# Products with V as 64-row tiles of the weight array, two key halves at a time, with the half query chunk widened to 128 columns

## The chip, the cores and the metric

One core of one Trainium2 chip. The metric is the device time of one launch in microseconds (us); lower is better. The engines are TensorE (PE; its weight loads are listed apart as PEld), VectorE (DVE), ScalarE (ACT), GpSimd (POOL) and the queue engine SP.

## The reference

Attention with one added to the softmax's denominator, over 8 batches x 12 heads, 448 tokens, head size 64; then a soft mixture of experts over all 3584 tokens with 8 experts of 4 slots each.

```python
# attention, per batch and head
scores = scale * q @ k.T                       # scale = 1/8
m = max(scores, axis=-1)
e = exp(scores - m)
x = (e / (sum(e) + exp(-m) + 1e-9)) @ v        # tokens go on as rows [3584, 768]
# soft MoE
logits = x @ phi                               # [3584, 32]
d = softmax(logits, axis=0); c = softmax(logits, axis=1)
slot_in = d.T @ x                              # [32, 768], 4 slots per expert
slot_out = relu(slot_in[e] @ w1[e]) @ w2[e]    # w1 768x1024, w2 1024x768
out = c @ slot_out
```

## The kernel before

Heads are worked in 48 pairs (`NPAIR`); a pair n holds two heads, hl = 0 in partitions 0 to 63 and hl = 1 in 64 to 127. The 448 tokens make three chunks of 128 and a half chunk of 64, for keys (index i) and for queries (index u). The order of all engines' work is the order in which the Python code issues it (`manual_schedule`): each engine runs its own part of that order strictly in sequence, and waits on the semaphore of whoever made its input or still uses its buffer.

For each pair there are these pieces:

- `T` (L241): 28 transposes of 64x64 turn q and k of a later pair into `ps_t`, copied out by ACT or DVE.
- `A` (L274): scores with queries on the partitions, only for the row maximum; `ps_a`, reduced by DVE (L287, L307). Seven reductions a pair.
- `W1` to `W3` (L310 to L349): once in three pairs the negated maxima are transposed to a row `mT`, and exp(-m) is made in `ec`.
- `Bk(n, i)` (L352): scores with keys on the partitions, plus the bias -m by a second matmul of 64 rows (L370, L399), then exp on ACT (L372, L402) into one of five SBUF buffers `e2` (both heads of a chunk side by side, 448 columns each) or, for the half chunk, into `e1`. The matmuls of the two heads use rows 0 to 63 and 64 to 127 of the array and stand alternately with those of `A`.
- `AV(n, i, qs)` (L421): the product with V. The exponentials are the weights (128 keys x 128 queries), V with a column of ones is the moving operand (65 columns). Per pair 4 key chunks x 4 query chunks x 2 heads = 32 matmuls; the half query chunk gives matmuls with 64 weight columns, the half key chunk stacks both heads' 64 keys on 128 rows with zeros in `vp` for the other head. All goes into one PSUM bank (`ps_av`, 7 x 65 columns).
- `N1` (L443): ACT copies `ps_av` to `ubuf`. `N2` (L452): DVE adds exp(-m) and takes the reciprocal, POOL multiplies in three operations (L469, L479, L480) into `x`.
- `PX` (L494): four matmuls with the identity transpose x; ACT copies them out (L507).
- `P(b)` (L516): the MoE's part for a batch, in six functions that the table `post` hangs into later half steps.

In the main loop a step s has two halves. The first: Bk(s,0), Bk(s,1), each with one `A` between; then AV(s-1) for key chunks 2 and 3, and the half query chunk of AV(s-1); N1. The second: Bk(s,2), Bk(s,3) with `A`; T(s+6); AV(s) for key chunks 0 and 1; PX(s-2); N2. The first three pairs are issued by hand, by the words of `ramp`; the MoE's expert layers and the output follow after the loop. PSUM has 8 banks: 3 in `psA`, 4 in `psB` (scores, `T`, `PX`), 1 in `psV` (`ps_av`).

POOL issues the loads of q, k, v and of the expert weights between its own work (`slot_loads`, `load_half`, `load_rows`); the tables `half_at`, `rows_at` and `stage_at` say in which step.

Of the kernel before, what the change touches and what calls it, by code (L numbers as in the profile page):

```python
# [24 lines left out]
HG = 6  # L25
NP = 3
# [5 lines left out]
def kernel(  # L32
# [37 lines left out]
    ident2 = const.tile([128, 128], BF16, name="ident2")  # L70
    ones = const.tile([128, 2], BF16, name="ones")
    sel = const.tile([128, HG], BF16, name="sel")
    phi_sb = const.tile([128, KC, NS], BF16, name="phi_sb")
    halfm = const.tile([128, 2], F32, name="halfm")
# [6 lines left out]
    sizes = [("nq0", 2 * NP * S), ("nq1", 2 * NP * S), ("nv", NATV), ("qk6", 2 * S), ("wm1", 512),  # L81
             ("qk0", 2 * S), ("qk1", 2 * S), ("qk2", 2 * S), ("wm0", 512), ("xTa", 4 * 512), ("qk3", 2 * S),
             ("vp0", VPN), ("x0", 4 * DD), ("qk4", 2 * S), ("qk5", 2 * S), ("e2", NE * 2 * S), ("e1", S),
# [12 lines left out]
    e1_t = part("e1", 0, S)  # L96
    vp = [part(f"vp{i}", 0, VPN).rearrange("p (h i d) -> p h i d", h=HG, i=4) for i in range(2)]
    wm = [part(f"wm{i}", 0, 512).rearrange("p (i c) -> p i c", i=4) for i in range(2)]
# [57 lines left out]

    with ExitStack() as at:
# [4 lines left out]
        psB = pool("psB", 4, space=PSUM)  # L162
# [3 lines left out]
        ubuf = pu.tile([128, 2, 7 * W65], F32, name="ubuf")  # L166
# [30 lines left out]
        for t in wm:  # L197
            nc.vector.memset(t, 0.0)
# [9 lines left out]
        for t, x in ((halfm, 1.0), (nhalfm, -1.0)):  # L208
            nc.vector.memset(t, 0.0)
            for hl in range(2):  # L210
                nc.vector.memset(t[64 - 64 * hl:128 - 64 * hl, hl:hl + 1], x)
        nc.vector.memset(ones, 1.0)
        nc.vector.memset(ones[64:128, 1:2], 0.0)
# [4 lines left out]
        for h in range(2):  # L218
            nc.vector.tensor_add(ident2[:, 64 * h:64 * h + 64], ident[:, 0:64], ident[:, 64:128])
# [11 lines left out]
        mx, ngm, ec, mT, eT, av, us = {}, {}, {}, {}, {}, {}, {}  # L231
# [9 lines left out]
        def T(n):  # L241
            g, pl = divmod(n, NP)
            first = n < NP * NP
            ps = psB.tile([128, 2, S], BF16, tag="b", name="ps_t")
# [65 lines left out]
        def W1(g):  # L310
            w, m = wm[g % 2], mx[g]
            l0, l1 = mpl(g)
            nm = psm.tile([128, 21], BF16, tag="ngm", name="ngm")
            neg = lambda o, s: nc.gpsimd.tensor_scalar(o, s, -1.0, None, op0=ALU.mult)
            cols = lambda t: t[:, 0:3 * HG].rearrange("p (i c) -> p i c", i=3)[:, :, 2 * l0:2 * l1]

            o = w[:, 3, :].rearrange("p (d c) -> p d c", d=2)[:, :, 2 * l0:2 * l1]
            nc.gpsimd.tensor_mul(
                o.rearrange("p d (l h) -> p d l h", h=2),
                m[:, 3 * HG + l0:3 * HG + l1].unsqueeze(1).unsqueeze(3).to_broadcast([128, 2, l1 - l0, 2]),  # L320
                nhalfm.unsqueeze(1).unsqueeze(1).to_broadcast([128, 2, l1 - l0, 2]))
            o = w[:, 0:3, :].rearrange("p i (d c) -> p i d c", d=2)[:, :, :, 2 * l0:2 * l1]
            neg(o, cols(m).unsqueeze(2).to_broadcast([128, 3, 2, 2 * (l1 - l0)]))
            if l1 - l0 == NP:
                neg(nm, m)
            else:
                nc.gpsimd.memset(nm, 0.0)
                neg(cols(nm), cols(m))
                neg(nm[:, 3 * HG + l0:3 * HG + l1], m[:, 3 * HG + l0:3 * HG + l1])
            ngm[g] = nm  # L330

        def W2(g):
            w = wm[g % 2]
            ps = pb_("ps_m")
            for i in range(3):
                nc.tensor.matmul(ps[:, i * 128:(i + 1) * 128], w[:, i, :], ident, start=True, stop=True)
            nc.tensor.matmul(ps[:, 384:448], w[:, 3, :], ident2[:, 0:64], start=True, stop=True)
            st["ps_m"] = ps

        def W3(g):  # L340
            t = psm.tile([128, S], BF16, tag="mT", name="mT")
            nc.scalar.copy(t, st["ps_m"][:, 0:S])
            mT[g] = t
            e = psm.tile([128, NP, 7], F32, tag="ec", name="ec", bufs=3)
            nc.scalar.activation(e[:, :, 0:6].rearrange("p l (i h) -> p i l h", i=3),
                                 ngm[g][:, 0:18].rearrange("p (i l h) -> p i l h", i=3, h=2),
                                 AF.Exp, scale=scale)
            nc.scalar.activation(e[:, :, 6], ngm[g][:, 18:21], AF.Exp, scale=scale)
            ec[g] = e  # L349


        def Bk(n, i, c=0, mix=False):  # L352
# [3 lines left out]
            rs = [slice(0, 64), slice(64, 128)]  # L356
            if i < 3 and mix and runs and runs[0][1] < 3:

                e = e2_t[st["e2"] % NE]
                st["e2"] += 1  # L360
                cols = slice(i * 128, (i + 1) * 128)
                a0, a1 = A(*runs.pop(0), steps=True)
                pss = {}

                def score(hl):
                    pss[hl] = pb_("ps_b")
                    nc.tensor.matmul(pss[hl][:, 0:S], t[rs[hl], 1, cols], t[rs[hl], 0, :], start=True, stop=False)  # L367

                def bias(hl):
                    nc.tensor.matmul(pss[hl][:, 0:S], sel[rs[hl], 2 * pl + hl:2 * pl + hl + 1].to_broadcast([64, 128]),  # L370
                                     mT[mg(n)][rs[hl], :], start=False, stop=True)
                    nc.scalar.activation(e[:, hl, :], pss[hl][:, 0:S], AF.Exp, scale=scale)  # L372
                    eT[n, i, hl] = e[:, hl, :]

                a0()
                score(1)
                score(0)
                bias(1)
                bias(0)
                a1()  # L380
                return
            if i < 3:
                pss = [pb_("ps_b") for _ in range(2)]
                outs = [p[:, 0:S] for p in pss]
                cols = slice(i * 128, (i + 1) * 128)
                e = e2_t[st["e2"] % NE]
                st["e2"] += 1
                es = [e[:, hl, :] for hl in range(2)]
            else:
                pss = [pb_("ps_b")]  # L390
                outs = [pss[0][r, 0:S] for r in rs]
                cols = slice(384, 448)
                es = [e1_t]
            m = cols.stop - cols.start
            for hl in range(2):
                nc.tensor.matmul(outs[hl], t[rs[hl], 1, cols], t[rs[hl], 0, :], start=True, stop=False)  # L396
            As(c)
            for hl in range(2):
                nc.tensor.matmul(outs[hl], sel[rs[hl], 2 * pl + hl:2 * pl + hl + 1].to_broadcast([64, m]), mT[mg(n)][rs[hl], :],  # L399
                                 start=False, stop=True)  # L400
            for p, e in zip(pss, es):
                nc.scalar.activation(e, p[:, 0:S], AF.Exp, scale=scale)  # L402
            for hl in range(2):
                eT[n, i, hl] = es[hl % len(es)]
# [10 lines left out]
        def av_tile(n):  # L415

            if n >= NPAIR - 3:
                return psA.tile([128, 512], F32, tag="a", name="ps_av")
# [613 lines left out]
```

## Time and profile before

| | |
|---|---|
| median of 3 runs | 299.27 us (299.16, 299.27 and 453.81) |
| span of the profiled execution | 299.0 us |
| PE busy | 271.4 us, 91% |
| DVE busy | 249.7 us, 84% |
| ACT busy | 249.8 us, 84% |
| POOL busy | 195.9 us, 66% |
| granted PE clock | 1.00 up to 270 us, 0.60 and 0.50 in the last 29 us |
| DMA | 58.7 MB in 299 us |

The span is the time from the first to the last instruction in the one execution that the profiler took; it is 0.3 us below the median. A group's line in the profile gives the source line, engine, operation, output<-input with shapes (for PE rows*columns of the weight tile first), the count, the busy time, the mean length of one in ns and the idle time before it. A line of the timeline gives the start in us, the time from the first start to the last end, and what ran. A matmul's length includes the way through the array, so that matmuls overlap: 448 columns last 0.35 us, but follow each other at 0.19 us.

### The profile page before, as it was taken

The numbers are of one execution on the slowest core, as the hardware profiler recorded it, in microseconds if no ns is written. First come the engines' busy times: TensorE is split into PE (matmuls) and PEld (weight loads), VectorE is DVE, ScalarE is ACT, GpSimd is POOL, SyncE is SP. The second block draws the span as 40 slices with busy tenths as digits, with TensorE's granted clock in tenths as the row PEclk, the third lists the DMA queues.
The fourth block names the chain that finished last, engine by engine and source line by source line (L and its number), as shares of the span: only waits on it lengthen the run. The fifth ranks groups of instructions, "written<-read, shape, count | busy, mean of one in ns | idle before, by whom it ended". The sixth has DMA issues, their size and how long they took to land.

```text
span 299.0 us, 12398 instructions
## 1 busy us (share of the span) xinstructions
PE 271.4 (91%) x5174; PEld 162.5 (54%) x5174; DVE 249.7 (84%) x581; ACT 249.8 (84%) x559; POOL 195.9 (66%) x391
## 2 busy tenths in 40 slices
PE   5999899999999999999899999999999999996820
PEld 4445456566666566566556666656665555652100
DVE  5899799999999989999889999998999675537930
ACT  3569999999899989998989899989999987337820
POOL 8792887979696979887879697978686633000000
PEclk9999999999999999999999999999999999997555
DMA  7999998999999999999999999999799989908997
GB/s 132 147 143 208 149 138 138 188 165 188 185 204 179 184 176 202 163 182 182 202 159 184 176 199 152 196 183 196 125 150 187 213 185 263 344 10 318 380 453 322
DMA packets 47015, 58.67 MB, mean 196 GB/s; under 512 B 2800, under 2 KB 39920, under 8 KB 46704
## 3 DMA queue, kind: packets, MB, share of 16 engines
q0 software_dynamic: 40304, 42.29, 89.6%
q1 hardware_dynamic: 6656, 15.60, 13.8%
q8 instruction: 40, 0.66, 0.8%
q14 instruction: 15, 0.12, 0.1%
HBM read 89.16 MB, written 15.14 MB: 349 GB/s over the span
## 4 chain that ended last, share of the span: by engine, by line
PE 68%; ACT 10%; DVE 6%; POOL 6%; issue 4%; DMA 2%; DVEq 0%; POOLq 0%; ACTq 0%
PE ps_av L436 15%; PE ps_a L285 10%; PE ps_b L367 7%; PE ps_b L370 7%; PE ps_t L256 5%; PE ps_b L396 5%; PE ps_x L501 3%; PE ps_b L399 3%; ACT W L402 2%; PE ps_o L925 2%; DVE mx L298 2%; PE ps_s L623 2%; PE ps_h L862 2%; PE ps_so L882 2%; ACT W L263 2%
## 5 line engine op out<-in xcount | busy, mean ns | idle before, releaser
L287 DVE TENSOR_REDUCE mx<-ps_a 128x1 f32<-128x448 f32 x250 | 137.3, 613 | 4.6 <-PE ps_a L285 3.5
L372 ACT ACTIVATE W<-ps_b 128x448 bf16<-128x448 f32 x250 | 120.4, 574 | 0.0
L285 PE MATMUL ps_a<-W 64*128 64x448 bf16 x250 | 80.9, 352 | 0.0
L367 PE MATMUL ps_b<-W 64*128 64x448 bf16 x250 | 70.5, 352 | 1.1
L436 PE MATMUL ps_av<-W 128*128 128x65 bf16 (+1 forms) x1536 | 64.9, 196 | 2.2 <-issue 1.6
L436 PEld LDWEIGHTS <-W 128*128 128x128 bf16 (+1 forms) x1536 | 50.5, 100 | 30.2 <-issue 26.4
L370 PE MATMUL ps_b<-mT,sel 64*128 64x448 bf16 x250 | 66.5, 350 | 0.0
L469 POOL TENSOR_TENSOR W<-ubuf,rec 128x384 bf16<-128x384 f32 x44 | 36.3, 824 | 35.7 <-ACT W L507 19.3
L402 ACT ACTIVATE W<-ps_b 128x448 bf16<-128x448 f32 x86 | 46.1, 574 | 2.0 <-PE ps_b L399 2.0
L256 PEld LDWEIGHTS <-W 64*64 64x64 bf16 x1344 | 29.3, 112 | 12.7 <-issue 4.3
L507 ACT CAST W<-ps_x 128x512 bf16<-128x512 f32 x47 | 28.6, 608 | 7.4 <-PE ps_x L501 7.2
L256 PE MATMUL ps_t<-ident,W 64*64 64x64 bf16 x1330 | 30.6, 195 | 2.4 <-ACT W L215 1.4
L307 DVE TENSOR_REDUCE mx<-ps_a 128x1 f32<-128x448 f32 x48 | 29.5, 615 | 1.4 <-PE ps_a L304 1.4
L285 PEld LDWEIGHTS <-W 64*128 64x128 bf16 x250 | 23.4, 94 | 9.8
L114 POOL DMA_DIRECT2D W<-in_moe_w_dram x30 | 22.6, 755 | 7.9 <-PE ps_b L399 7.8
L370 PEld LDWEIGHTS <-sel 64*128 64x128 bf16 x250 | 19.6, 94 | 14.4 <-issue 5.6
L396 PE MATMUL ps_b<-W 64*64 64x448 bf16 (+1 forms) x134 | 27.1, 374 | 0.3
L449 ACT COPY ubuf<-ps_av 128x455 f32<-128x455 f32 x44 | 25.1, 571 | 0.8 <-POOL W L408 0.6
L399 PE MATMUL ps_b<-mT,sel 64*64 64x448 bf16 (+1 forms) x134 | 25.1, 354 | 0.1
L263 ACT COPY W<-ps_t 128x896 bf16<-128x896 bf16 x21 | 19.5, 927 | 6.5 <-PE ps_t L256 6.5
L298 DVE TENSOR_REDUCE mx<-ps_a 128x1 f32<-128x448 f32 x38 | 21.1, 616 | 1.9 <-PE ps_a L294 1.9
L480 POOL TENSOR_TENSOR W<-ubuf,rec 128x128 bf16<-128x128 f32 x44 | 17.5, 398 | 3.7
(156 smaller groups left out, 446.6 us busy)
## 6 DMA issues: line engine op xcount, KB each, us to landing
W<-in_moe_w_dram POOLq DMA_DIRECT2D x24, 768.0 KB, 9.9
W<-in_v_dram POOLq DMA_DIRECT2D x32, 192.0 KB, 6.5
out_dram<-W SPq DMA_DIRECT2D x2, 2688.0 KB, 10.0
W<-in_q_dram POOLq DMA_DIRECT2D x15, 336.0 KB, 6.3
W<-in_k_dram POOLq DMA_DIRECT2D x15, 336.0 KB, 7.5
stage<-in_moe_w_dram POOLq DMA_DIRECT2D x4, 768.0 KB, 9.6
W<-stage SPq DMA_DIRECT2D x4, 576.0 KB, 7.3
out_dram<-W SPq DMA_DIRECT2D x6, 384.0 KB, 3.0
```

Source lines behind the costliest of these rows:

```text
L256: nc.tensor.transpose(o, src[r, pl, tok * D:(tok + 1) * D], ident[r, r])
L285: nc.tensor.matmul(ps[:, 0:S], t[r, 0, i * 128:(i + 1) * 128], t[r, 1, :], start=True, stop=True)
L287: nc.vector.reduce_max(m[:, c:c + 1], ps[:, 0:S], axis=AX.X)
L307: nc.vector.reduce_max(mx[g][:, c:c + 1], ps[:, 0:S], axis=AX.X)
L367: nc.tensor.matmul(pss[hl][:, 0:S], t[rs[hl], 1, cols], t[rs[hl], 0, :], start=True, stop=False)
L370: nc.tensor.matmul(pss[hl][:, 0:S], sel[rs[hl], 2 * pl + hl:2 * pl + hl + 1].to_broadcast([64, 128]), mT[mg(n)][rs[hl], :], start=False, s ...
L372: nc.scalar.activation(e[:, hl, :], pss[hl][:, 0:S], AF.Exp, scale=scale)
L396: nc.tensor.matmul(outs[hl], t[rs[hl], 1, cols], t[rs[hl], 0, :], start=True, stop=False)
L399: nc.tensor.matmul(outs[hl], sel[rs[hl], 2 * pl + hl:2 * pl + hl + 1].to_broadcast([64, m]), mT[mg(n)][rs[hl], :], start=False, stop=True)
L402: nc.scalar.activation(e, p[:, 0:S], AF.Exp, scale=scale)
L436: nc.tensor.matmul(o, eT[n, i, hl][:, qc], vp[g % 2][:, 2 * pl + hl, i, 0:W65], start=(i == 0 and u == 0 and hl == 0) or (u == 3 and i == ...
L469: eng.tensor_mul(x[:, 0:3, c:c + 128].rearrange("p i (h d) -> p i h d", h=2), u[:, 0:6, 0:D].rearrange("p (i h) d -> p i h d", h=2), rec[: ...
```

## The change

The product with V is made with the array in the shape of the scores, 64 rows x 128 columns. Pass 0 (`AV(n, 0)`) takes head 0's keys of the rows 0 to 63 beside head 1's keys of the rows 64 to 127, each head into a PSUM bank of its own; pass 1 takes the other halves. Key chunk 3 (64 keys of each head) needs pass 0 alone. So a pair has 32 + 24 = 56 matmuls. The half query chunk becomes 128 columns: its weights run on into the 64 columns that lie behind the 448 in SBUF (`e_cols`), which are the first columns of the next exponentials; the 64 extra result rows are masked in the MoE by a matmul with `twin` that adds -1e30 to their logits. The last pair uses `AV_last`, 32 matmuls of 128 rows.

PSUM becomes `psA` 3, `psB` 3, `psV` 1 tile of two banks; `T`, `W2` and `W3` move from `psB` to `psA`. `N1` copies 2 x 260 columns; `N2` is one POOL multiplication. exp(-m) is made from `mT` by four small matmuls and one exp. `wm` has one buffer. `Bk` becomes `X` (chunks 0 to 2) and `H` (half chunk), the step is written as one sequence, the ramp and some places of `post` and `rows_at` are new.

```diff
-        psB = pool("psB", 4, space=PSUM)
+        psB = pool("psB", 3, space=PSUM)
...
-    ubuf = pu.tile([128, 2, 7 * W65], F32, name="ubuf")
+    ubuf = pu.tile([128, 2, 8 * W65], F32, name="ubuf")
...
+    e_cols = lambda e, hl, u: (part("e1", 0, S + 64) if e < 0 else part("e2", (2 * e + hl) * S, S + 64))[:, u * 128:u * 128 + 128]
...
-            ps = psB.tile([128, 2, S], BF16, tag="b", name="ps_t")
+            ps = (psB if n == 0 else psA).tile([128, 2, S], BF16, tag="b" if n == 0 else "a", name="ps_t")
...
         def W3(g):
...
+            ps = psA.tile([128, 4, HG], F32, tag="a", name="ps_e")
+            for i in range(4):
+                nc.tensor.matmul(ps[:, i, :], mT[g][:, i * 128:i * 128 + 128], ident[:, 0:HG], start=True, stop=True)
+            e = ec[g] = psm.tile([128, 4, HG], F32, tag="ec", name="ec", bufs=3)
+            nc.scalar.activation(e, ps, AF.Exp, scale=scale)
...
+        def X(n, i, mix=False, between=()):
...
+            z = st["e2"] % NE
+            st["e2"] += 1
...
+            def expo(hl):
+                nc.scalar.activation(e2_t[z][:, hl, :], pss[hl][:, 0:S], AF.Exp, scale=scale)
+                eT[n, i] = z
+
+            for f in runs_[0:1]:
+                f()
+            score(1)
+            score(0)
+            bias(1)
+            bias(0)
...
-        def AV(n, i, qs):
+        def AV(n, phase):
...
+            if n not in av:
+                t = psV.tile([128, 2, 512], F32, tag="v", name="ps_av")
+                av[n] = [t[:, hl, :] for hl in range(2)]
+                av[n, 2] = t
+            for i in (0, 1, 3, 2) if phase == 0 else (0, 1, 2):
+                for u in range(4):
+                    for r in range(2):
+                        hl = r ^ phase
+                        nc.tensor.matmul(av[n][hl][:, u * W65:u * W65 + W65], e_cols(eT[n, i], hl, u)[rs[r]],
+                                         vp[g % 2][rs[r], 2 * pl + hl, i, 0:W65], start=(phase == 0 and i == 0 and u == 0),
+                                         stop=(phase == 1 and i == 2), skip_group_check=True)
...
+                    if j == 0:
+                        nc.tensor.matmul(v["ps_l"][:, 3, :], twin, ident[:, 0:1].to_broadcast([128, NS]),
+                                         start=False, stop=False, skip_group_check=True)
...
-                at_z = (0, 1, 2, 4, 5, 9) if late(b) else (0, 1, 2, 3, 4, 6)
+                at_z = (1, 3, 5, 6, 7, 9) if late(b) else (0, 1, 2, 3, 4, 6)
...
-        runs = [(n, i) for n in range(NPAIR) for i in (0, 3, 1, 2)]
+        runs = [(n, i) for n in range(NPAIR) for i in (3, 0, 1, 2)]
...
+        for s in range(3, NPAIR):
+            mix = len(runs) > 1
+            X(s, 0, mix)
+            AV(s - 1, 0)
+            for f in post.get(2 * s, ()):
+                f()
+            X(s, 1, mix)
+            if s + 1 in firsts:
+                W1(mg(s + 1))
+            late_loads(s)
+            if s < NPAIR - 6:
+                T(s + 6)
+            H(s, int(mix))
+            for f in post.get(2 * s + 1, ()):
+                f()
+            PX(s - 2)
+            if s in firsts:
+                W3(mg(s))
+            if s + 1 in firsts:
+                W2(mg(s + 1))
+            if s < NPAIR - 6:
+                AV(s - 1, 1)
+                N1(s - 1)
+                X(s, 2, len(runs) > 0)
             else:
+                X(s, 2, len(runs) > 0, [lambda: AV(s - 1, 1)])
+                N1(s - 1)
+            N2(s - 1)
+            end_loads(s)
```

## The prediction

> **What bounds the kernel now.** I read the page's busy times first, then the busy times of the steady stretch from 45 to 245 us, then the timeline of one step, engine by engine.
>
> ```profile
> PE 271.4 (91%) x5174; PEld 162.5 (54%) x5174; DVE 249.7 (84%) x581; ACT 249.8 (84%) x559; POOL 195.9 (66%) x391
> ...
> L372 ACT ACTIVATE W<-ps_b 128x448 bf16<-128x448 f32 x250 | 120.4, 574 | 0.0
> L285 PE MATMUL ps_a<-W 64*128 64x448 bf16 x250 | 80.9, 352 | 0.0
> ...
> L436 PE MATMUL ps_av<-W 128*128 128x65 bf16 (+1 forms) x1536 | 64.9, 196 | 2.2 <-issue 1.6
> ```
> ```profile
> 45.00:245.00 200.00, 195.57 (x3930) 122.24 (x3926) 184.19 (x430) 190.29 (x442) 159.16 (x308) 1.00 1.11 179
> ```
>
> No single engine sets the pace: in the stretch PE is busy 98%, ACT 95%, DVE 92%. From the copy N1 of pair 2 (46.4 us) to that of pair 43 (246.1 us) a pair takes 4.87 us. What each needs of these is read from the timelines.
>
> ```profile
> 122.41 0.52 PE L370 MATMUL ps_b<-mT,sel 64*128 64x448 bf16 x2
> 123.42 0.60 PE L256 MATMUL ps_t<-ident,W 64*64 64x64 bf16 x28
> 123.95 0.54 PE L436 MATMUL ps_av<-W 128*128 128x65 bf16 x12
> 124.33 0.39 PE L501 MATMUL ps_x<-ident,W 128*128 128x128 bf16 x4
> 124.65 0.36 PE L285 MATMUL ps_a<-W 64*128 64x448 bf16 x1
> 124.65 0.55 PE L367 MATMUL ps_b<-W 64*128 64x448 bf16 x2
> 124.85 0.54 PE L370 MATMUL ps_b<-mT,sel 64*128 64x448 bf16 x2
> 125.23 0.73 PE L367 MATMUL ps_b<-W 64*128 64x448 bf16 x2
> ```
> ```profile
> 120.67 1.85 ACT L372 ACTIVATE W<-ps_b 128x448 bf16<-128x448 f32 x4
> 122.39 0.57 ACT L449 COPY ubuf<-ps_av 128x455 f32<-128x455 f32 x1
> 122.86 0.98 ACT L372 ACTIVATE W<-ps_b 128x448 bf16<-128x448 f32 x2
> 123.72 0.55 ACT L402 ACTIVATE W<-ps_b 128x448 bf16<-128x448 f32 x1
> 124.15 0.93 ACT L263 COPY W<-ps_t 128x896 bf16<-128x896 bf16 x1
> 124.93 0.63 ACT L507 CAST W<-ps_x 128x512 bf16<-128x512 f32 x1
> ```
>
> An exp holds ACT 0.43 (120.67 to 122.39 for four), but its result is there only 0.57 after its start. So ACT's work per pair is 7 x 0.43 + PX 0.48 + N1 0.42 + `T` 0.79 in a third of the pairs + `W3` (0.43 + 0.21)/3 + the MoE's 0.73/6 = 4.5; ACT idles about 0.4 of 4.87. On PE, two 448-column products in the two halves of the rows run together: 124.65 to 124.85, 0.19 to 0.20 for two.
>
> **The change, part by part.**
>
> *Removed: changes of array shape.* The last transpose of 123.42 starts at 123.83 (0.60 less one length, 0.19); the next group starts 0.12 later where transposes follow at 0.03: 0.09 lost. The same after PX (124.33 + 0.17 to 124.65, less 0.06). Before, a step changes shape six times (scores, AV, half-chunk AV, scores, H and T, AV and PX, scores), after it three times (T and H, PX, AV): -0.28 us per pair, up to -13 us in all if PE alone set the pace.
>
> *The product itself.* Before: 12 matmuls from 123.95 to 124.33, 0.031 each, 32 in about 0.97. After: 28 couples of 64-row tiles. No row shows such a couple. Lower bound: both halves together as the scores and the 28 transposes do (14 couples in 0.41, 0.029 each): 0.83. Upper: one after the other, 56 x 0.031 = 1.74. I take 0.83: loads of 64 x 128 weights for both halves stand within 0.02 us:
>
> ```profile
> 144.26 0.09 PEld L285 LDWEIGHTS <-W 64*128 64x128 bf16 x1
> 144.26 0.11 PEld L367 LDWEIGHTS <-W 64*128 64x128 bf16 x2
> 144.28 0.28 PEld L370 LDWEIGHTS <-sel 64*128 64x128 bf16 x2
> ```
>
> *Small moves.* N1 copies 520 columns for 455: +0.06 on ACT. N2: POOL 0.81 + 0.37 + 0.34 becomes about 0.81 x 512/384 = 1.08, hidden under POOL's idle third. `W3`: two exps (0.21) become one (about 0.12), `mT` +0.06, once in three pairs: nothing. The seven mask matmuls, the ramp and DMA issues in another step: nothing; the loads are the same bytes, and POOL has less work before them. At the end all 32 products of the last pair wait for its exps, before only 20: +0.4.
>
> *Added: a wait that empties ACT.* The widened half chunk reads 64 columns behind head 1's exponentials. For key chunk 2 these belong to the e2 buffer that the next pair's X(s,0) has just been given, and pass 0 of AV(s-1) comes right after X(s,0). The instruction list of the changed kernel shows it: in 36 of the 47 pairs the last weight load of pass 0 waits for the second exp of X(s,0), the newest instruction that ACT has; in the other pairs the buffer is the last of the five and the columns are those of `e1`. PE works strictly in order, so the scores X(s,1), `T`, H and PX stand behind that load, and ACT, DVE and POOL behind them. Price: from the exp's start 0.57 to its result, 0.05 to PE (PX's copy ends 125.56, the score that needs its bank, second of 125.23, runs at 125.62), 0.03 for the last product, 0.20 until the bias of X(s,1) starts (124.65 to 124.85), 0.35 for it, 0.10 to ACT (122.76 to 122.86) = 1.30, less the 0.43 that ACT is at work: ACT stands idle 0.87. On the average of pairs 0.87 x 36/47 = 0.67.
>
> *Fewer banks.* With three in `psB`, the second score of one X waits for the first exp of the X before: 0.57 + 0.05 + 0.35 + 0.10 = 1.07 after that exp's start, against 2 x 0.43 of work: 0.21 idle, between X(s-1,2) and X(s,0), where nothing else lies. Bounds 0 (if PX's or N1's copy is late and fills it) to 0.21 plus the same in the pairs without the wait, 0.05; I take 0.21. Then H's exp: after the restart, X(s,1), a change, `T`, H take PE 0.56 + 0.09 + 0.40 + 0.37, so the exp comes about 0.2 after ACT has done X(s,1), unless ACT copies `T`: 0 to 0.2, I take 0.1.
>
> In three of five pairs a load of pass 1 waits in the same way for H's exp, where the columns of `e1` lie behind; that exp is done about when pass 1 starts: 0 to 0.1, I take 0.
>
> *Sum per pair.* ACT's work 4.5 + 0.06 and idle time 0.67 + 0.21 + 0.1 make 5.54, 0.67 over the 4.87 of before. PE's saving of 0.28 lies inside PE's waits now. From the 0.67 I take off 0.05, as the MoE's copies fill part of the bank gap: 0.62 x 43 pairs = 26.7. DVE, 4.6 per pair of its own (seven reductions of 0.53, its copies of `T`, the reciprocals, the MoE), keeps up.
>
> *Instruction fetch.* PE's program grows from 10,343 to 12,785 instructions.
>
> ```profile
> q8 instruction: 40, 0.66, 0.8%
> ...
> 143.26 0.38 PE L256 MATMUL ps_t<-ident,W 64*64 64x64 bf16 x12 [0.60 <-issue]
> ```
>
> 40 packets of 16 KB are 40 blocks of 256 instructions. By the packets' times each starts 0.3 to 4.4 us after PE enters the block before, late when the data queues are full, and the new block can run 2.3 to 2.5 us after that. Four came too late: stops of 0.8, 1.3, 0.5 and 0.7, in the middle of the transposes above, 3.2 in all. A block lasts 6.2 us now; with 241 instead of 192 instructions a pair it would last 5.8 at 5.5 us a pair, and by the same delays 40 fetches would lose 7; most falls into the waits above. I take 2, bounds 0 and 7. The Trainium skill (Runtime: NRT & Kernel Launch, Instruction fetch mechanics) calls the crossing of a block mostly hidden; by that the sum would be 2 lower. The trace disagrees, with these four stops.
>
> Sum: 299.0 (span of the profiled execution, 0.3 under the median) + 26.7 + 2 + 0.4 = 328.
>
> **The rivals.**
>
> *Faster: the drains decide (289).* If ACT's idle time after the wait were already in the 0.4 it has now, and PE's six changes the true limit, a pair would fall to DVE's own work, 4.65: 299 - 0.22 x 43 = 289. For it: PE 98% busy, and the clean steps now run at 4.6. Against: ACT's work alone is 4.5, and a load that waits for the newest exp leaves ACT nothing to do. It decides only if the wait is under 0.2, that is if the exp is done when pass 0 ends.
>
> *Nothing (302).* Wait on ACT half hidden (0.35 a pair, +15) and the changes of shape paid back in full (-13).
>
> *Fetch as the bound (310).* If the wait hides, blocks of 256 still need the larger of 4.7 and the fetch: over the 30 delays of the steady stretch 5.45 on the average, 5.13 per pair: +0.26 x 43 = +11.
>
> *The couples don't overlap (341).* +0.9 of PE per pair; pass 0's half hides in the wait, pass 1 delays N1 by 0.3 more: +13. Against: the rows of scores and loads. The Trainium skill (TensorE: Matmul & The Clock Gate, LDWEIGHTS (loading the stationary operand)) gives a load columns / 1.2 ns, 107 ns here; end to end, 28 in each half would cost 3 us a pair, 2.2 more than now, and the time would pass 390; I give that under 0.01 of this rival's chance. The rows disagree: 12 loads and products in 0.38.
>
> **How the numbers follow.** Forecast 0.65, couples apart 0.09, fetch alone 0.13, nothing 0.08, faster 0.05. Low end: only the wait, 4.56 + 0.67 = 5.23, +15, and fetch alone 310: 309. High end: 5.6 per pair, fetch 7, and part of the couples' case: 341. The first three are slower by over 2% (what a measurement here can tell): 0.87.
>
> **What would show it.** In the profile after: weight loads of `ps_av` that wait for ACT's exp, about 0.5 us in 36 pairs; ACT idle 0.9 us at a time before X(s,1), and under 88% busy in the steady stretch; PE busy falling too; a pass 0 of 32 in about 0.5 apart from its last; more stops by issue. Wrong if ACT stays 95% busy, or if N1 follows N1 at under 5.1 us.

## The result, and the profile after

The changed kernel takes 348.26 us (median of 4 runs, 347.44 to 349.86) against 299.22 us: a ratio of 1.168, 95% interval 1.163 to 1.172. It is slower, as forecast, but by 49 us where 29 were forecast, and outside the range of 309 to 341. The profiled execution took 347.44 us, with a span of 345.6. A run that came out over 1.5% above the fastest of its kernel (one of 453.81 us before) is left out of all ratios and intervals, but not of the medians.

The page of the changed kernel, the lines that answer to those of before:

```profile
PE 274.9 (80%) x6395; PEld 167.5 (48%) x6395; DVE 254.8 (74%) x574; ACT 261.5 (76%) x542; POOL 172.6 (50%) x283
...
L363 ACT ACTIVATE W<-ps_b 128x448 bf16<-128x448 f32 x288 | 142.2, 551 | 31.7 <-PE ps_b L357 29.0
L354 PE MATMUL ps_b<-W 64*128 64x448 bf16 x288 | 83.6, 354 | 21.3 <-ACT W L363 19.8
...
L414 PE MATMUL ps_av<-W 64*128 64x65 bf16 x2632 | 66.4, 190 | 18.0 <-ACT W L363 14.1
```

The third field is the idle time ahead of the group. Before, the exps stood at 0.0, and the scores that they read at 1.1:

```profile
L367 PE MATMUL ps_b<-W 64*128 64x448 bf16 x250 | 70.5, 352 | 1.1
```

Now ACT waits 29.0 us for scores, and PE waits 19.8 + 14.1 us for exps. Each waits for the other. The steady stretch, engine by engine:

```profile
45.00:245.00 200.00, 165.87 (x4329) 106.41 (x4329) 164.91 (x368) 172.29 (x364) 122.60 (x190) 1.00 0.99 153
```

PE has gone from 195.57 to 165.87 us busy, ACT from 190.29 to 172.29 (86%), DVE from 184.19 to 164.91. All three stand idle more, and none is the bound. The page also follows the work that ended last back from release to release (its chain) and gives each engine's share of it:

```profile
PE 68%; ACT 10%; DVE 6%; POOL 6%; issue 4%; DMA 2%; DVEq 0%; POOLq 0%; ACTq 0%
ACT 44%; PE 37%; issue 7%; DVE 6%; DMA 1%; DVEq 0%; ACTq 0%; POOL 0%; POOLq 0%
```

The first line is of the kernel before, the second of the changed one: the chain now passes from ACT to PE and back. Of the list of waits, the last two lines below are the predicted wait; the first was not predicted:

```profile
DVE mx L290 <- PE ps_a L288: 37.5, 69, 1.4
...
ACT W L363 <- PE ps_b L357: 29.0, 43, 1.6
PE ps_b L354 <- ACT W L363: 19.8, 42, 0.6
PEld L414 <- ACT W L363: 18.4, 36, 0.5
...
PE ps_av L414 <- ACT W L363: 14.1, 36, 0.4
```

The columns are total us, number, longest. 36 weight loads of `ps_av` wait for the newest exp. DVE waits 37.5 us for row-maximum scores; before it was 3.5 us in 10 waits. The timeline of PE, then of ACT, in one pair:

```profile
123.00 0.35 PE L354 MATMUL ps_b<-W 64*128 64x448 bf16 x1
123.91 0.35 PE L354 MATMUL ps_b<-W 64*128 64x448 bf16 x1 [0.56 <-ACT W L363]
...
124.29 0.64 PE L414 MATMUL ps_av<-W 64*128 64x65 bf16 x31
125.35 0.20 PE L414 MATMUL ps_av<-W 64*128 64x65 bf16 x1 [0.42 <-ACT W L363]
```
```profile
123.27 2.02 ACT L363 ACTIVATE W<-ps_b 128x448 bf16<-128x448 f32 x4
126.02 0.98 ACT L363 ACTIVATE W<-ps_b 128x448 bf16<-128x448 f32 x2 [0.73 <-PE ps_b L357]
```

The second score of X(s,0) waits 0.56 for a bank; 31 products of pass 0 run, the last waits 0.42 for the exp; ACT then stands 0.73 until X(s,1).

Where the 46.6 us between the two spans are, by the starts of the exps (seven a pair; "pair 3" is the start of the first exp of X(3,0), before of Bk(3,0)):

| stretch | before | after | difference |
|---|---|---|---|
| start to pair 3 | 33.95 | 39.58 | +5.6 |
| pairs 3 to 42, each | 4.885 | 5.707 | +0.82, in 39 pairs +32.0 |
| pair 42 to the last exp | 25.6 | 32.7 | +7.1 |
| last exp to the end | 48.9 | 50.7 | +1.9 |

### The profile page after: what moved, and what is told of

Read it like the earlier page. It is cut to its first block, busy times and chain, and to the rows that moved or that the text cites. A ratio compares the mean times of both kernels' runs of the same rounds, so it can differ in the third digit from the quotient of the medians.

```text
span 345.6 us, 14663 instructions
## 1 busy us (share of the span) xinstructions
PE 274.9 (80%) x6395; PEld 167.5 (48%) x6395; DVE 254.8 (74%) x574; ACT 261.5 (76%) x542; POOL 172.6 (50%) x283
## 4 chain that ended last, share of the span: by engine, by line
ACT 44%; PE 37%; issue 7%; DVE 6%; DMA 1%; DVEq 0%; ACTq 0%; POOL 0%; POOLq 0%
ACT W L363 23%; ACT ubuf L435 7%; PE ps_t L259 6%; PE ps_av L414 5%; ACT W L391 5%; ACT W L484 5%; PE ps_b L354 4%; PE ps_b L357 3%; PE ps_a L288 3%; DVE mx L290 2%; PE ps_b L386 2%; PE ps_s L602 2%; PE ps_o L891 2%; PE ps_b L389 2%; PE ps_h L828 2%
## 5 line engine op out<-in xcount | busy, mean ns | idle before, releaser
L290 DVE TENSOR_REDUCE mx<-ps_a 128x1 f32<-128x448 f32 x250 | 142.3, 611 | 37.8 <-PE ps_a L288 37.5
L363 ACT ACTIVATE W<-ps_b 128x448 bf16<-128x448 f32 x288 | 142.2, 551 | 31.7 <-PE ps_b L357 29.0
L354 PE MATMUL ps_b<-W 64*128 64x448 bf16 x288 | 83.6, 354 | 21.3 <-ACT W L363 19.8
L458 POOL TENSOR_TENSOR W<-ubuf,rec 128x512 bf16<-128x512 f32 x44 | 46.4, 1055 | 92.7 <-DVE rec L456 55.1
L414 PE MATMUL ps_av<-W 64*128 64x65 bf16 x2632 | 66.4, 190 | 18.0 <-ACT W L363 14.1
L357 PE MATMUL ps_b<-mT,sel 64*128 64x448 bf16 x288 | 74.8, 355 | 0.0
L414 PEld LDWEIGHTS <-W 64*128 64x128 bf16 x2632 | 55.2, 94 | 35.4 <-ACT W L363 18.4
L310 DVE TENSOR_REDUCE mx<-ps_a 128x1 f32<-128x448 f32 x48 | 29.7, 620 | 3.8 <-PE ps_a L307 3.5
L391 ACT ACTIVATE W<-ps_b 128x448 bf16<-128x448 f32 x48 | 26.6, 554 | 4.1 <-PE ps_b L389 4.1
L435 ACT COPY ubuf<-ps_av 128x520 f32<-128x520 f32 x44 | 26.8, 608 | 0.4
L288 PEld LDWEIGHTS <-W 64*128 64x128 bf16 x250 | 23.4, 94 | 4.8 <-issue 1.1
L301 DVE TENSOR_REDUCE mx<-ps_a 128x1 f32<-128x448 f32 x38 | 21.8, 619 | 4.0 <-PE ps_a L297 3.5
L354 PEld LDWEIGHTS <-W 64*128 64x128 bf16 x288 | 18.0, 94 | 5.1 <-issue 2.2
L478 PE MATMUL ps_x<-ident,W 128*128 128x128 bf16 x192 | 18.8, 219 | 0.6 <-DVE W L458 0.5
L307 PE MATMUL ps_a<-W 64*64 64x448 bf16 x96 | 18.9, 386 | 0.4 <-DVE W L264 0.4
```

What stands on the lines that cost most here:

```text
L288: nc.tensor.matmul(ps[:, 0:S], t[r, 0, i * 128:(i + 1) * 128], t[r, 1, :], start=True, stop=True)
L290: nc.vector.reduce_max(m[:, c:c + 1], ps[:, 0:S], axis=AX.X)
L310: nc.vector.reduce_max(mx[g][:, c:c + 1], ps[:, 0:S], axis=AX.X)
L363: nc.scalar.activation(e2_t[z][:, hl, :], pss[hl][:, 0:S], AF.Exp, scale=scale)
L391: nc.scalar.activation(e1_t, ps[:, 0:S], AF.Exp, scale=scale)
L414: nc.tensor.matmul(av[n][hl][:, u * W65:u * W65 + W65], e_cols(eT[n, i], hl, u)[rs[r]], vp[g % 2][rs[r], 2 * pl + hl, i, 0:W65], start=(ph ...
```

## The experiments

All were timed beside the kernel before, which took 298.2 to 299.3 us in the five series; ratios are to it. "Idle ahead of" an instruction of ACT is worked out from the starts, as the distance from the start before less the short distance (10th percentile) after that kind. Idle times are averages over the pairs 3 to 42. Each result has the ratio with its 95% interval and, where it says something, the length of a steady pair (3 to 42).

### The wait for the newest exp

**Taken out of the changed kernel.** `e2` has five buffers (the expectation says three); each gets 64 zero columns of its own.

```diff
-    e_cols = lambda e, hl, u: (part("e1", 0, S + 64) if e < 0 else part("e2", (2 * e + hl) * S, S + 64))[:, u * 128:u * 128 + 128]
+    e_cols = lambda e, hl, u: (part("e1", 0, S + 64) if e < 0 else part("e2", e * (2 * S + 64) + hl * S, S + 64))[:, u * 128:u * 128 + 128]
...
+        for z in range(NE):
+            nc.vector.memset(part("e2", z * (2 * S + 64) + 2 * S, 64), 0.0)
```

> The changed kernel with one thing different: each of the three buffers that hold the exponentials of a full key chunk is followed by 64 zero columns of its own, so the 128 columns that the half query chunk now takes never reach into the next buffer, which the newest exponentials are just being written to. Nothing else of the order or the number of instructions changes. Theory W (the wait of the V products for the newest exponential, found in 36 pairs, is the main loss): that wait goes from the trace; ScalarE's idle time ahead of the exponentials that followed it falls from 0.62 to about 0.2 us per pair, 0.41 x 40 = 16 us in the steady pairs, and some us more in the ramp and in the last six pairs: about 327 us (324 to 332). Rival F (the 2400 more instructions of TensorE have to be fetched, and that is what costs): nothing that it names changes, 344 to 348. Rival B (three banks of scores in place of four are the loss): the wait only moves to the bank, 340 to 348.

Measured 339.01 us, 1.136 (1.132 to 1.141); 5.459 per pair. The waits of the V products are gone, but only 9 us came back, little more than half of the 16 that theory W expected at least, and the time lies between the ranges of W and B. ACT's idle time ahead of X(s,1) fell from 0.66 to 0.27 us, as said; ahead of X(s,0) it rose from 0.17 to 0.21 and ahead of H from 0.18 to 0.25, and PE still waits for banks:

```profile
PE ps_b L355 <- ACT W L364: 19.3, 40, 0.7
```

What stood behind the wait shows in the chain of this kernel. DVE, with 6% in the changed kernel, now has 24%, most of it row-maximum reductions:

```profile
PE 44%; DVE 24%; ACT 18%; issue 6%; DMA 3%; POOL 0%; DVEq 0%; ACTq 0%; POOLq 0%
```

**Put alone into the kernel before.**

```diff
                     for i in (2, 3):
                         AV(s - 1, i, range(3))
+                    if s < NPAIR:
+                        nc.tensor.matmul(av[s - 1][:, 500:502], eT[s, 1, 0][:, 0:128], vp[0][:, 0, 0, 0:2],
+                                         start=False, stop=True, skip_group_check=True)
```

> The kernel before, with one small product more in each pair: 128 rows, 2 columns, behind the V products of key chunks 2 and 3 in the first half step, with the newest exponential of key chunk 0 as its weights, written to columns of the V products' bank that nothing reads. It gives the kernel before the wait that the change added, and none of the rest of the change: four score banks, the old shapes, the old number of products. Theory W: ScalarE is idle 0.6 to 0.9 us more per pair, times 43: 325 to 335 us. Rivals F and B: the wait is hidden by the scores that lie ready, 299 to 303.

Measured 341.94 us, 1.145 (1.143 to 1.147), above the 325 to 335 of theory W; 5.595 per pair. The added load waits in 42 pairs:

```profile
PEld L780 <- ACT W L372: 31.0, 42, 0.9
```

So one such wait costs 44 us in a kernel that has no other, and 9 in the changed one. It stands here ahead of N1, a different place from the change's, so its 44 is not that wait's price; it shows what draining ACT once a pair can cost.

### The banks

**Before with three score banks.** `psB` from 4 to 3, nothing else.

> The kernel before with psB cut from four banks to three; the eighth bank stays empty, and order, shapes and products are those of before. Theory B (what is left of the loss once the wait for the newest exponential is gone comes mostly from the bank that the second V bank took): ScalarE stands idle 0.2 us and more at one or two places of a pair, 0.25 to 0.5 us per pair: 310 to 322 us. Rival O (it is the new order of the step that costs, transposes, half chunk, transposed x and pass 1 in one row without scores, then three score groups in a row): with the order of before three banks are nearly enough, 299 to 304.

Measured 320.5 us, 1.070 (1.063 to 1.076); 5.303 per pair, +0.42. Theory B holds in the order of before.

**Both losses in before.** The small product and three banks.

> The kernel before with both single losses at once: the small product that waits for the newest exponential (alone 341.9, +43) and three banks of scores (alone 320.5, +21). If the losses add: 361 to 366 us. If they overlap, because an engine that stands still for the one reason can't stand still for the other at the same time: 342 to 352 us; that would be why the wait, taken out of the changed kernel, gave back only 9 us.

Measured 354.54 us, 1.187 (1.181 to 1.192). The two alone make 44 + 21 = 65; together 56. They overlap, but by 9 us, between what the two theories expected. That isn't enough to explain why the wait gave back only 9.

**Four score banks at the cost of `psA`.** In the changed kernel with zero columns, `psA` 2 and `psB` 4.

> The changed kernel with the zero columns behind each buffer, and with the banks divided as 2 in psA and 4 in psB in place of 3 and 3 (the last batch of the mixture and a part of the output layers then take their banks from psB). Theory B: the idle time before the second exponential groups (0.21 and 0.27 us per pair with the zero columns) goes, less what the row maxima lose with two banks: 320 to 329 us against 339. Rival O: within 3 us of 339, or slower, as VectorE then waits for its banks.

Measured 366.27 us, 1.223 (1.214 to 1.232). Theory B missed; it came out as rival O's "or slower", but by 27 us: 5.880 per pair, and pair 3 starts only at 50.62 (41.01 with the zero columns alone). Between 60 and 245 us PE now waits 8.6 us ahead of row-maximum scores and 5.8 ahead of transposes for DVE to free a `psA` bank; with the zero columns alone it was 0.9. With late transposes besides:

> The zero columns, the transposes behind X(s,2), and 2 banks in psA with 4 in psB, all three. If banks and order are two separate losses: steady pairs at 4.8 to 4.95 us and 308 to 318 us in all. If they are two names for one (either of them lets TensorE go on while ScalarE is busy): no better than the better of the two alone by more than 4 us. If psA with two banks becomes the limit: VectorE waits for the row-maximum scores, and it is slower than the order alone.

Measured 364.34 us, 1.217 (1.208 to 1.226): the third case, `psA` as the limit. So `psA` has no bank to spare in this kernel.

**Releasing PE earlier inside X.** Zero columns, and `bias(1)` ahead of `score(0)`.

> The changed kernel with the zero columns behind each buffer, and with the shift row of the second head issued ahead of the first head's scores, so that the exponential of the second head can begin without the third of the three score banks. Theory W plus bank (the rest of the idle time is the wait of the second score for a bank, 0.2 us between key chunk 2 and key chunk 0 of the next pair and, with the zero columns, as much in the next step): both gaps shrink, 0.3 to 0.4 us per pair off the kernel with the zero columns alone: 310 to 318 us. If the bank isn't it: within 3 us of that kernel, or slower by the two more changes of form between scores and shift rows.

Measured 336.82 us, 1.128 (1.123 to 1.133), within 3 us of the zero columns alone. The idle time ahead of X(s,0) went (0.21 to 0.03), and came back ahead of X(s,1) (0.27 to 0.35) and H (0.25 to 0.33). PE still sits at the second score until the bank is free, 32 times and 10.1 us between 60 and 245.

### The order of the step

**Transposes moved, end order changed.** Zero columns; T(s+6) behind X(s,2); pass 1 and N1 ahead of X(s,2) in the last six pairs too.

```diff
-                X(s, 2, len(runs) > 0, [lambda: AV(s - 1, 1)])
-                N1(s - 1)
+                AV(s - 1, 1)
+                N1(s - 1)
+                X(s, 2, len(runs) > 0)
```

> The changed kernel with the zero columns, and two changes of order in different stretches of time. In the pairs up to 41 the transposes T(s+6) stand behind X(s,2) instead of between X(s,1) and H: TensorE makes them where it now waits 0.45 us for a score bank, and the stretch without scores becomes shorter. In the last six pairs pass 1 and N1 stand ahead of X(s,2), as in the others, instead of inside it. Theory O: 0.35 us per pair less in the steady pairs (5.46 to about 5.1, -13 us), and 3 to 4 us less in the last six: 320 to 326 us. Theory B: the bank sets the pace in any order, 5.4 us per pair and more, 334 to 340 us.

Measured 333.24 us, 1.112 (1.103 to 1.122). The last six pairs gave 3.4 us (33.6 to 30.1), as expected; a steady pair only 0.08 (5.459 to 5.379) of the 0.35 that theory O expected. PE's wait for a score bank is nearly gone (1.8 us for 16.1 between 60 and 245), but PE now stops without a wait; from the waits between 40 and 255 us:

```profile
PE ps_av L415 <- issue: 4.7, 6, 1.7
PE ps_t L260 <- issue: 3.6, 4, 1.4
```

Between 45 and 250 us there are 12 such stops, 9.1 us in all, each exactly 256 products and weight loads (or a multiple) from the next, each 2.2 to 2.5 us after a packet of the instruction queue started. In the kernel before there are 4, of 2.5 us in all; in the changed kernel one, of 0.5 (a further 0.6 stands at a block's start, but is put down to DVE); with the zero columns 6, of 5.3.

**The same with 32 products of 128 rows**, two banks for V.

> The kernel with zero columns, transposes behind X(s,2) and the usual order in the last six pairs (333 us), with 32 products of 128 rows in place of 56 of 64, eight of each pass's chunks (0 and 1, then half chunk and 2), still into two banks and with three for the scores. In that kernel's trace TensorE stands still without a wait, at the head of new blocks of instructions, for 8 to 9 us between 40 and 255 us. Theory F2 (once the waits for exponentials are gone, the fetch of instructions shows through): 1100 instructions and as many loads less take these stops away, and of the 8 us come back those that two to three more changes of shape per pair (0.09 each, 0.18 to 0.27 x 39 = 7 to 10 us if all of it counted) don't eat: 326 to 333 us, with the stops under 2 us. Rival: the stops have another cause and stay, 336 to 343 us.

Measured 337.03 us, 1.127 (1.122 to 1.133); 5.464 per pair. The stops are gone, all of them, yet it is slower by some 4 us. It has two changes of shape more a pair, but also a wait that the couples don't have: its half chunk is in pass 1, behind H, and between 60 and 245 us products wait 5.5 us for H's exp, in 12 pairs. What each of the two took isn't told apart. The same product with the zero columns alone, and the half chunk in pass 0 as in the change:

> The changed kernel with the zero columns behind each buffer, and with the products of a pair as 32 of 128 rows in place of 56 of 64 rows (key chunks 0, 1 and the half chunk in the first pass, key chunk 2 in the second), so with some 1100 products and as many weight loads less, and two changes of shape more per pair. Theory W with the price of a change of shape from the traces (0.09 us): TensorE is not what ends the chain, so within 4 us of the kernel with the zero columns alone, 323 to 331. Rival F: the missing instructions bring 5 us and more against it.

Measured 343.96 us, 1.150 (1.145 to 1.155), 5 us slower than with couples; 5.632 per pair. The 5 us and more that rival F expected the other way did not come; two changes of shape more a pair are in this number too.

**Half steps with couples.** X(s,0), X(s,1), pass 0; X(s,2), H, T, pass 1, PX, N1.

> The changed kernel with the zero columns and the couples in their two passes, in half steps near those of before: X(s,0), X(s,1), pass 0; then X(s,2), H, T, pass 1, transposed x, N1. Three score banks. Theory O (the new order of the step is the larger part of what is left): near the kernel before with three banks, 5.1 to 5.3 us per pair, 325 to 332 us against 339. Theory R (the rest of the change or the bank in any order): 336 us and more.

Measured 362.8 us, 1.213 (1.206 to 1.219); 6.087 per pair. Theory O missed; theory R's "336 us and more" holds, but it doesn't say why the time should lie 24 us over that of the zero columns alone. This order, with N1 at the very end, isn't that of before; between 60 and 245 us DVE waits 32.1 us for `ubuf`. It shows only how much an order can cost.

**The ramp.** Late transposes and end order, with T0 to T8 in `psB`, E0 and E1 later.

> The kernel with zero columns, transposes behind X(s,2) and the usual order in the last six pairs (333 us), with two changes before the steady pairs only: the transposes T0 to T8 take their bank from psB, as before, and exp(-m) of the first two groups is made later (E0 behind X(0,0), E1 behind the half chunk of pair 1), where TensorE need not wait for ScalarE's copy of the maxima. Theory (the ramp's 5.6 us are waits of TensorE for banks in psA and for this copy): the first exponential of pair 3 comes at 35 to 37 us in place of 39.5, 328 to 331 us in all. Rival (VectorE's maxima set the ramp): within 1 us of 39.5, no change in all.

Pair 3 starts at 36.49 instead of 39.52: 3 of the ramp's 5.6 us are banks of `psA` and the wait for the copied maxima. The whole is 333.04 us, 1.107 (1.099 to 1.115) against 1.112 (1.103 to 1.122): the intervals overlap, and its runs spread from 328.74 to 334.23, so the 3 us can't be told in the whole.

### Back to before, step by step

The 32 products of 128 rows run one after the other and go into one bank here, so these kernels have four score banks (where no other number is said) with the rest of the change kept. To fit into the bank, all of them leave out the last eight result columns of the second head's half query chunk, seven of V and the sum.

**The new order, old product, four banks.**

```diff
-        psB = pool("psB", 3, space=PSUM)
+        psB = pool("psB", 4, space=PSUM)
...
-                t = psV.tile([128, 2, 512], F32, tag="v", name="ps_av")
+                t = psV.tile([128, 512], F32, tag="v", name="ps_av")
...
-            for i in (0, 1, 3, 2) if phase == 0 else (0, 1, 2):
+            for i in (0, 1) if phase == 0 else (3, 2):
```

> The order of the changed kernel with the zero columns, but the products as 32 matmuls of 128 rows (key chunks 0 and 1 in pass 0, half chunk and chunk 2 in pass 1), which can all go to one bank: psV one bank, psB four. Eight columns of the second head's half query chunk, which no longer fit into the bank, are left out. So it has the new order and all four score banks, and not the new shape. Theory B (the bank is the largest part of the loss, and it is the price of the couples, since two row halves at work together need two banks): steady pairs from 5.46 to about 5.0, 315 to 324 us. Rival O (the order of the step): 334 to 344 us, with or without the bank.

Measured 333.66 us, 1.117 (1.111 to 1.124); 5.476 per pair: no better than the couples with three banks in a steady pair; the 5 us are in the last six pairs (28.5 for 33.6) and the ramp (39.0 for 41.0). But this kernel can't decide on theory B. Its half chunk has moved to pass 1, behind H(s), which has by then written the next pair's exponentials into the one buffer `e1`. So pass 1 takes those, and waits for them, which the kernel with the zero columns never does:

```profile
PEld L415 <- ACT W L392: 12.7, 25, 0.9
```

With late transposes and the end order, and the same wait:

> As the kernel with one V bank, four score banks and 128-row products (the same eight columns left out), with the transposes behind X(s,2) and the order of the last six pairs as in the others. Theory B: the order brings as much as it did with three banks, 0.08 us per pair and 3.4 us in the last six pairs: 6 us below the kernel with one V bank, 309 to 317 us. If the order matters more once there is a bank to run ahead into: 303 to 309 us.

Measured 330.08 us, 1.106 (1.099 to 1.113), above both expectations, and 7 us below the same with three banks (337.03), which has that wait too. So a bank is worth 7 us in this order, not the 15 to 24 that theory B expected of it.

**The order of before, old product, four banks.**

```diff
+            X(s, 0, mix)
+            X(s, 1, mix)
+            AV(s - 1, 0, (3, 2))
...
+            AV(s - 1, 1, (3, 2))
+            N1(s - 1)
...
+            X(s, 2, len(runs) > 0)
+            H(s, int(len(runs) > 0))
+            if s < NPAIR - 1:
+                AV(s, 0, (0, 1))
+            if s < NPAIR - 6:
+                T(s + 6)
```

> The step's order of before (key chunks 2 and 3 with N1 in the first half step, chunks 0 and 1 in the second), 32 products of 128 rows into one V bank and four score banks, the last eight columns of the second head's half query chunk left out; but all the rest of the change: transposes and exp(-m) in psA, copies of 512 columns, one POOL multiplication, the masks, the new ramp, the half query chunk as 128 columns. Theory O: the steady pairs are back at 4.8 to 4.95 us, and 302 to 309 us in all, with the new ramp's 5 us. Theory R: 5.2 us and more per pair, 318 to 330 us.

Measured 318.38 us, 1.067 (1.064 to 1.071); 5.177 per pair. That is at the edge of theory R, not in theory O's range. It is 15 us less than in the new order, but the half chunk stands ahead of H again, so the order and the wait for H's exp went together. With three banks:

> As the kernel in the order of before with 128-row products, one V bank and the same eight columns left out, with three score banks in place of four; one bank stays empty. If a bank costs in this order what it cost in the kernel before (0.42 us per pair): 16 to 20 us more than with four banks. As the transposes now take their bank from psA, it may be half as much: 8 to 12 us more.

Measured 332.32 us, 1.113 (1.107 to 1.120); 5.450. Here a bank is worth 14 us, between the two expectations. This kernel also gives the order without the wait for H: beside the 128-row products in the new order with three banks and the half chunk in pass 0 (343.96, 5.632) it is 12 us faster.

**T and W2 directly behind H**, ahead of the V products, and the ramp as above.

> The kernel in the order of before with 128-row products, one V bank and four score banks (the same eight columns of the second head's half query chunk left out), with T and W2 directly behind H, ahead of the V products, as before, and the ramp with the transposes in psB and the later E0 and E1. Theory O (the order, down to the place of the transposes, is what costs): the steady pairs at 4.8 to 4.95 us, the ramp 3 us shorter, 302 to 307 us against 318. Theory R (the rest of the change costs 0.3 us per pair): only the ramp's 3 us, 314 to 317 us.

Measured 309.48 us, 1.037 (1.032 to 1.043), between the two theories; 5.016 per pair, the ramp 3.2 us shorter. Two fewer changes of shape and an earlier copy of the maxima: 0.16 per pair. **And the transposes in `psB`:**

> As the kernel with T directly behind H, with the bank of all transposes in psB, as before. If psA, with row-maximum scores, maxima and transposes in three banks, holds TensorE up: 2 to 5 us faster than with the transposes in psA. If it doesn't: within 1.5 us, or slower, as the scores then lack the bank.

Measured 306.41 us, 1.022 (1.012 to 1.032); 4.904 per pair, that of before within 0.02. What is left is the ramp: pair 3 starts at 38.04, 4.1 late. None of the kernels beats before.

The walk from before to after, by kernels without the wait for H's exp. Those of 306.41 to 343.96 us have the 32 products, and all of them but the last leave out the eight columns:

| step | us | ratio | steady pair |
|---|---|---|---|
| before | 298.2 to 299.3 | 1 | 4.885 |
| rest of the change: copies, masks, one POOL operation, ramp | 306.41 | 1.022 | 4.904 |
| transposes take `psA`'s banks | 309.48 | 1.037 | 5.016 |
| transposes behind V products, maxima later, first ramp | 318.38 | 1.067 | 5.177 |
| three score banks | 332.32 | 1.113 | 5.450 |
| the new order of the step, with a second V bank | 343.96 | 1.150 | 5.632 |
| couples | 339.01 | 1.136 | 5.459 |
| the wait for the newest exp | 348.26 | 1.168 | 5.707 |

The intervals of neighbours don't meet, except for those of the second and third line, which just touch. The steps are +8, +3, +9, +14, +12, -5 and +9 us. The 14 us of the bank are near the forecast (0.21 + 0.1 in 43 pairs, 13). Each price holds in this sequence only: put alone into the kernel before, a wait for the newest exp cost 44, and a bank 21.

What the order does is seen in the fifth and sixth line of the table. First the steady stretch of each (of the order of before, then of the new one; the fields after the window are PE, PEld, DVE, ACT, POOL), then waits of each between 60 and 245 us. The order of before has one of the three, the new one all:

```profile
45.00:245.00 200.00, 193.34 (x3650) 114.04 (x3646) 172.80 (x386) 177.81 (x383) 125.69 (x196) 1.00 1.00 159
45.00:245.00 200.00, 174.90 (x3503) 105.50 (x3502) 168.63 (x374) 174.24 (x371) 122.23 (x191) 1.00 0.99 155
```
```profile
DVE mx L291 <- PE ps_a L289: 7.0, 19, 0.6
```
```profile
DVE mx L291 <- PE ps_a L289: 26.7, 61, 0.9
PE ps_b L355 <- ACT W L364: 18.8, 33, 0.6
ACT W L364 <- PE ps_b L358: 17.6, 33, 0.6
```

In the new order six of the seven row-maximum scores and six of the seven exps of a pair come in one stretch, X(s,2), X(s+1,0), X(s+1,1), with only pass 0 between; then PE does T, the mixture, PX and the other pass with one of each. In the first stretch PE runs into full score banks (18.8 us, 33 times; the list of the order of before has no such wait); in the second DVE and ACT run dry (26.7 us of DVE against 7.0). DVE's idle time isn't the price: in this kernel DVE has 4% of the chain, PE 55% and ACT 30%. That the bunching is what costs is read from these lines and not shown; spreading the exps or the row-maximum scores over the new order wasn't tried. Nor were couples in the very order of before: there the two passes follow each other closely, and the second sends a head's products into the bank that the other half of the rows has just been writing. The Trainium skill (TensorEngine Tiling (Array Packing), Gotcha 1: PSUM Pressure) says that different row tiles can't use one bank at the same time and that software has to keep them apart; no run here shows it.

## Why the prediction was wrong in size

**The step that failed** is the sum: what lies outside three named idle times of a steady pair it set to nothing, or charged like a steady pair. By the table of stretches, the 46.6 us are 17.5 over the 29.1 that were forecast: +7.8 in the 39 steady pairs (0.82 for 0.62 each), +5.6 in the ramp, +4.6 in the last six pairs, +1.5 at the end, -2 for the fetch, which has no place of its own in the table.

**The wait itself: right in place, wrong in price.** 36 pairs, 0.4 to 0.5 us of PE each, ACT idle 0.84 at the median ahead of X(s,1) for 0.87, 0.66 per pair for 0.67. But "Price" took ACT's idle time as the kernel's loss. Taking the wait out gave 0.25 per pair back: the bank's 0.2 stood right behind it, as the text itself had for "the pairs without the wait", ACT's idle time ahead of H grew, and DVE's reductions came into the chain.

**Fewer banks: right in place.** 0.17 us between X(s-1,2) and X(s,0) for 0.21, ahead of H 0.18 for 0.1. In the order of before a bank costs 14 to 21 us.

**The sum per pair.** ACT's work is 4.45 by the distances of its starts, not 4.56; its idle time is 1.25, not 0.98. The three named places have 1.01 of it, near the forecast. The term that was too small is the rest, 0.24 (ahead of PX's copy, N1 and the mixture's): before, ACT stood idle 0.44 a pair, 0.33 of it in such places, and the sum let all of this vanish. 5.54 became 5.71, and counted from the base of before +0.82 in place of +0.62.

**"Small moves ... the ramp ... nothing": wrong.** The ramp is 5.6 us; in it the transposes' move to `psA`, which the text didn't price at all, cost about 3 together with the waiting exp(-m), and 0.11 per pair with four banks in the order of before. The last six pairs have an order of their own (V products inside X(s,2)), charged like the others: they lost 7.1, of which 3.4 by that order. The end lost 1.9 for 0.4.

**Left out: the order of the step.** No term and no rival named the order, though it costs 12 us alone in the walk, and the transposes' later place, with the ramp, another 9. So, by the prices of the walk, the sum came as near as it did by luck: 29 us (0.67 in 43 pairs) for a wait that gave back 9, and nothing for these, are two errors that partly offset each other. DVE "keeps up" holds in the changed kernel: it is busy 164.91 of 200 us, 4.7 of a pair's 5.71, and has 6% of the chain; it no longer holds once the wait is taken out (24%). The saving of changes of shape, six to three, bought nothing that shows: PE stands idle 34 of the 200 us.

**The rivals.** Couples apart is out: the 24 products of pass 1, 12 couples, start at 122.06 and the next group at 122.43, 0.031 a couple. The drains don't decide: three changes of shape instead of six came with a slower kernel, and five in the kernel of 306.41 us left the pair at 4.904. Fetch as the bound is out: the stops of the changed kernel are 0.5 to 1.1 us between 45 and 250. The 2 us taken for fetch had the wrong sign, as the 299.0 to which they were added held 2.5 us of stops there already. The bound of 7 was passed where the other waits were taken away (9.1). The Trainium skill's "mostly hidden" (Runtime: NRT & Kernel Launch, Instruction fetch mechanics) agrees with the changed kernel and not with the one of the 12 stops.

## What to carry to other kernels

Here three engines with 4.4 to 4.8 us of work in a step of 4.9 were held together by the order and the banks; a change that forces a new order has to be priced by what each engine has in hand in each stretch of it, not by the waits it adds. An idle time seen in the trace is a wait's price only if nothing stands right behind it: here 0.66 us in place were worth 0.25. To divide a loss, walk back to the old kernel one part at a time, and look in each step's trace for waits that the step itself brought in: a half chunk moved behind H made the order look 15 us dear, and without it the order cost 12. A part has no price of its own: the same bank was worth 21, 14 and 7 us in three orders.

## What the runs showed of the hardware

Products of 64 rows in both halves at once run at about 0.03 us per couple with 65 columns, as long as one product of 128 rows took before (0.031). Blocks of 256 products and weight loads begin 2.2 to 2.5 us after their packet of the instruction queue starts, in every stop that was read. Between 45 and 250 us one stop showed in the changed kernel, where TensorE waits for exps, and twelve in the kernel of 333.24 us with as many products, where those waits are gone.
